# One kernel of attention, routed experts and a SoLU layer: the overflow path moved behind the second layer, and the order inside the attention loop changed

## The chip, the core and the metric

The kernel runs on one core of one Trainium2 chip. The metric is the device time of one execution, in microseconds. A core has five engines that run their own instruction queues and meet through semaphores: TensorE (PE in the profile, PEld for its weight loads), VectorE (DVE), ScalarE (ACT), GpSimd (POOL) and SyncE (SP, which here only issues transfers). Transfers issued by SP or ACT are described in hardware; the scattered row transfers of this kernel are issued by GpSimd, one instruction for 128 rows.

## The reference

```python
for t in range(S):                                   # 2 batches, 8 heads, 768 steps, head size 40
    m_new = maximum(f[t] + m, i[t])
    f_stab, i_stab = exp(f[t] + m - m_new), exp(i[t] - m_new)
    C = f_stab * C + i_stab * outer(v[t], k[t])
    n = f_stab * n + i_stab * k[t]
    y[t] = sigmoid(o[t]) * (C @ q[t]) / maximum(abs(n @ q[t]), 1)
x = y as 1536 rows of 320
logits = x @ w_gate + log1p(exp(x @ w_noise)) * noise
top2 = the two largest of 8 experts; weights by softmax over the two
x = sum over the two: weight * (relu(x @ w1[e]) @ w2[e])       # 320 -> 1024 -> 320
h = x @ w_in; s = h * softmax(h); ln = (s - mean) / sqrt(var + 1e-6) * g
out = ln @ w_out
```

## The kernel before

The work has three stages: attention with routing (0 to 125 us of the profile), eight experts (to about 330 us), the SoLU layer (to the end).

**Attention** works on 12 tiles of 128 tokens, `i` = 0 to 11, two batches in turn, in a loop that is written out and software-pipelined by hand (manual schedule: the order of the calls is the order of each engine's queue). The loop of lines 679 to 718 runs over `i` = 4 to 10; the first tiles are written out ahead of it, and the last (`t` = 11) behind it. One turn `i` does on TensorE, in this order: `ranks(i-3)` (L449, L450), half of the scores of tile `i+1` with `update(i)` between two pairs of them (`scores`, L340; `update`, L368), `inter(i)` (L376, the state part of the output), the other scores, with `attend(i)` (L381, 41 columns per head) in two halves around a pair of scores and `trans(i-1)` (L415), then `logits(i-1)` (L425).

Around it, in the order of their queues:

- GpSimd: `rows` copies one column (L400), `keys(i+1)` makes the decayed queries and the decayed state (L350, L352), `send(i-3)` scatters the rows of a finished tile to its two experts' places in `xg` (two indirect transfers, L473, each behind a one-element memset, L472), and `causal(i+2)` masks the decay matrix `E` (L333). In turns 5, 7 and 9 it also makes the low half of one third of expert 0's first weights (`split_lo`, L121).
- VectorE: `rows(i-1)`, `route(i-2)` and `slot(i-3)` woven together (L401 to L457), `probs(i+1, 0)` (L344: `E` times scores), the keys with their weights (L357), `state(i)` (L391), `probs(i+1, 1)`.
- ScalarE: exponentials (L324, L329), copies of transposes (L419), the high halves of the weights.

Buffers tie the turns together: two PSUM buffers for the scores, so the scores of a tile wait for the `probs` of the tile before it; one PSUM buffer `U`, so `update(i+1)` waits for `state(i)`; four SBUF buffers for the rows `x`, so the copy L400 and the product L405 of `rows(4)` wait until both transfers of `send(0)` have landed.

`send(0)` is issued ahead of the loop (line 663), with `causal(5)` behind it in GpSimd's queue (line 675). It is the first indirect transfer of the program.

**Early rows.** The first 192 rows of expert 0 are complete when tile 7 is sent. They are read back (`early_load`), transposed (`early_turn`, L503), and put through expert 0's first layer (`early_mm`, 8 groups of 8 matmuls, L127 to L134) and most of its second (`early_out`, L149 to L154) while the last tiles are still being routed. `early_cut` (L139 on ScalarE, L140 and L142 on VectorE) takes a group of `early_mm` out of PSUM; the second-layer buffers of `early_out(0)` are those of groups 2 and 3, so it waits for both cuts. `split2(j)`, j = 3 to 6, makes the low half of a piece of expert 0's second weights on VectorE (L121) and issues the load of the next expert's piece. `busy` and `fill` issue matmuls on constant data whose result nobody reads.

**The overflow path.** Experts have fixed row counts (`CAPS`). `totals` (L769 to L774) writes into `cmi` whether any count is exceeded. Lines 803 to 861 load `cmi` into a register of every engine (L803) and branch on it (L804): if it is set, a general path recomputes all experts from all rows with plain loops. With the inputs timed it is skipped. In the kernel before it stands between the attention stage and the experts; what the fast path would write for the same rows is sent out of bounds by adding `flag` to its row numbers (L798 to L800, L974, L975).

## Time and profile before

| | us |
|---|---|
| median of 3 runs | 437.44 (437.33 to 437.52) |
| the execution that was profiled | 438.42 |
| its span, first to last instruction | 436.6 |
| mean granted TensorE clock | 0.963 |

The profile tells for each engine how long it was busy, in what order the work ran, and what ended each wait. The granted clock is given as a share of 2.4 GHz: 1.00 is that, 0.50 is 1.2 GHz. Times below are from the start of the span. A line of the timeline gives start, duration, engine, source line, operation, output and inputs, and in brackets how long the engine was idle before it and what the profile takes to have ended the wait. Where one wait is for several things, the one named is the last by the profile, which need not be the true one.

### The profile page before, as it was taken

What the parts mean: (1) busy time and instruction counts of PE and PEld (TensorE: products, weight loads), DVE (VectorE), ACT (ScalarE), POOL (GpSimd) and SP (SyncE); (2) the same over time, 40 slices, a digit from 0 to 9 for tenths busy, and PEclk for the clock granted to TensorE, in tenths of its full rate; (3) what the DMA queues carried; (4) which work ended last, traced back from release to release, by engine and by line L of the source; (5) the groups of instructions that cost most, each with busy time, mean ns of one, the idle gap of its engine ahead of it and who ended that gap; (6) DMA issues with size and microseconds to landing.
All of it is one profiled execution on the core that took longest, in us unless ns stands there. A gap on an engine that the chain in (4) does not pass through costs nothing.

```text
span 436.6 us, 8125 instructions
## 1 busy us (share of the span) xinstructions
PE 424.3 (97%) x2731; PEld 397.1 (91%) x2731; DVE 291.8 (67%) x736; ACT 242.9 (56%) x524; POOL 203.0 (46%) x284
## 2 busy tenths in 40 slices
PE   7999899999989999999999999999999999999996
PEld 4898799999979999999999999999897898999996
DVE  8897788677646368486585867756656875666541
ACT  4786826753137463663736547373835866656651
POOL 8582798984317443444435345362022543423330
PEclk9999958997699999999999999999999999999999
DMA  6879956955635859376594756736114112210001
GB/s 191 257 228 268 318 187 211 290 224 162 187 111 162 301 173 295 109 262 202 156 298 128 264 187 218 252 98 186 49 60 146 55 47 62 75 45 17 30 17 47
DMA packets 37538, 71.75 MB, mean 164 GB/s; under 512 B 4386, under 2 KB 19142, under 8 KB 37489
## 3 DMA queue, kind: packets, MB, share of 16 engines
q1 hardware_dynamic: 34336, 62.06, 45.5%
q0 software_dynamic: 2912, 8.68, 5.5%
q8 instruction: 24, 0.39, 0.4%
q10 hardware_dynamic: 240, 0.41, 0.3%
q14 instruction: 26, 0.20, 0.2%
HBM read 55.50 MB, written 16.21 MB: 164 GB/s over the span
## 4 chain that ended last, share of the span: by engine, by line
PE 70%; DVE 0%; ACT 0%; issue 0%; DVEq 0%; ACTq 0%
PE po L149 6%; PE po L151 6%; PE po L150 6%; PE ph L127 3%; PE cpo L1162 3%; PE cpo L1164 3%; PE cpo L1163 3%; PE ph L128 3%; PE ph L133 3%; PE ph L132 3%; PE ph L134 3%; PE ph L129 3%; PE ph L130 3%; PE ph L131 3%; PE pt L989 2%; PE pz L1154 2%
## 5 line engine op out<-in xcount | busy, mean ns | idle before, releaser
L121 POOL TENSOR_TENSOR w0l<-r,w0h 128x1024 fp32r<-128x1024 f32 x24 | 57.5, 2394 | 30.7 <-ACT w0h L117 27.5
L166 POOL DMA_INDIRECT yt<-YS,ti x29 | 31.2, 1075 | 86.1 <-ACT YS L164 55.7
L140 DVE SCALAR_TENSOR_TENSOR h<-ph,h 128x384 fp32r<-128x384 f32 (+1 forms) x64 | 34.6, 541 | 54.3 <-ACT h L139 54.3
L149 PE MATMUL po<-w1h,h 128*128 128x320 f32 x184 | 56.7, 308 | 0.0
L151 PE MATMUL po<-w1h,h 128*128 128x320 f32 x184 | 56.7, 308 | 0.0
L150 PE MATMUL po<-w1l,h 128*128 128x320 f32 x184 | 56.6, 308 | 0.0
L139 ACT ACTIVATE h<-ph 128x448 fp32r<-128x448 f32 (+6 forms) x64 | 32.2, 502 | 37.2 <-PE ph L134 32.0
L150 PEld LDWEIGHTS po<-w1l,h 128*128 128x128 f32 x184 | 34.6, 188 | 0.0
L149 PEld LDWEIGHTS po<-w1h,h 128*128 128x128 f32 x184 | 34.5, 188 | 0.0
L151 PEld LDWEIGHTS po<-w1h,h 128*128 128x128 f32 x184 | 34.5, 188 | 0.0
L473 POOL DMA_INDIRECT xg<-x,slots x24 | 25.8, 1076 | 18.2 <-DVE ix L441 6.2
L340 PE MATMUL S<-Qb,Kb 128*128 128x128 f32 x192 | 32.1, 305 | 0.6 <-DVE E L344 0.6
L121 DVE TENSOR_TENSOR w1l<-r,w1h 128x640 fp32r<-128x640 f32 x36 | 29.4, 821 | 2.6 <-ACT w1h L117 2.6
L1156 DVE TENSOR_TENSOR ZL<-pz,ZH 128x512 fp32r<-128x512 f32 x24 | 15.4, 685 | 22.6 <-ACT ZH L1155 22.6
L1162 PE MATMUL cpo<-w1h,ZH 128*128 128x320 f32 x96 | 30.0, 312 | 0.0
L1164 PE MATMUL cpo<-w1h,ZL 128*128 128x320 f32 x96 | 29.7, 310 | 0.0
L1163 PE MATMUL cpo<-w1l,ZH 128*128 128x320 f32 x96 | 29.7, 309 | 0.0
L164 ACT ACTIVATE YS<-po 128x320 f32<-128x320 f32 x20 | 8.8, 439 | 37.2 <-issue 31.1
L117 ACT ACTIVATE w0h<-r 128x1024 fp32r<-128x1024 f32 x27 | 28.2, 1050 | 0.0
L340 PEld LDWEIGHTS S<-Qb,Kb 128*128 128x128 f32 x192 | 26.9, 209 | 1.2 <-DVE E L344 1.0
L117 ACT ACTIVATE w1h<-r 128x640 fp32r<-128x640 f32 x36 | 25.5, 731 | 0.5 <-DMA r<-in_w_dram 0.5
L381 PEld LDWEIGHTS Y<-KV,E 128*128 128x128 f32 x192 | 25.1, 204 | 0.2
(264 smaller groups left out, 1249.7 us busy)
## 6 DMA issues: line engine op xcount, KB each, us to landing
r<-in_w_dram SPq DMA_DIRECT2D x24, 512.0 KB
r<-in_w_dram SPq DMA_DIRECT2D x32, 320.0 KB
E<-gd SPq DMA_DIRECT2D x8, 512.0 KB
X<-xg SPq DMA_DIRECT2D x7, 579.0 KB
KV<-in_kv_dram SPq DMA_DIRECT2D x12, 324.0 KB
cY<-yt SPq DMA_DIRECT2D x12, 320.0 KB
cvR<-in_win_dram SPq DMA_DIRECT2D x6, 512.0 KB
cvR<-in_wout_dram SPq DMA_DIRECT2D x5, 512.0 KB
```

The lines of the kernel that those rows point to most:

```text
L117: act.activation(splits[e][2 * m][:, k : k + n], raws[e, j], AF.Copy)
L121: eng.tensor_sub(splits[e][2 * m + 1][:, k : k + n], raws[e, j], splits[e][2 * m][:, k : k + n].bitcast(F32))
L139: act.activation(h[:, 0:n], ph, AF.Relu)
L140: ve.scalar_tensor_tensor(h[:, n + r : n + r + w], ph[:, 0:w], 0.0, h[:, 0:w].bitcast(F32), op0=ALU.max, op1=ALU.subtract)
L149: pe.matmul(po, hh, W2H[:, f], start=a, stop=False)
L150: pe.matmul(po, hh, W2L[:, f], start=False, stop=False)
L151: pe.matmul(po, hl, W2H[:, f], start=False, stop=z)
L166: i = pool.indirect_dma_start(out=yt, out_offset=bass.IndirectOffsetOnAxis(ap=idx[0:w], axis=0), in_=YS[0:w], in_offset=None, bounds_check ...
L340: pe.matmul(S[:, a], Kb[i % 3][j][:, a], Qb[i % 3][:, a], start=True, stop=True)
L1162: pe.matmul(po, ZH[:, f], W2H[:, f], start=(f == 0), stop=False)
L1163: pe.matmul(po, ZH[:, f], W2L[:, f], start=False, stop=False)
L1164: pe.matmul(po, ZL[:, f], W2H[:, f], start=False, stop=(f == 7))
```

## The change

Three things are done.

1. The overflow path moves to the end of the kernel, behind the last store. It now also recomputes the SoLU layer and writes the output itself, and its direct transfers are issued by GpSimd instead of SP. The `flag` arithmetic of the fast path goes; instead `positive` clears the sign bit of the row numbers (one VectorE instruction beside each `place`).
2. In the attention loop: `send(0)` moves behind `causal(5)`; `attend(i)` is cut into 2, 3 and 3 heads instead of 4 and 4, with a pair of scores between the first two cuts and behind the second; the three `split_lo` on GpSimd become six VectorE subtractions of 512 columns, one in each of the turns 5 to 10, behind `probs(i+1, 1)`; `busy(2)` of turn 9 goes.
3. Behind the loop: `attend(11)` is cut after 3 heads instead of 2; `busy(1)` comes behind it and `busy(2)` behind the `early_turn`s; `split2(3)` moves behind `send(t-1)`; `split2(4)` to `split2(6)` move behind `early_cut(1)` to `early_cut(3)`; `early_cut(0)` moves ahead of `slot(t)` and `totals`.

```diff
+    def positive(ti):
+        ve.tensor_scalar(ti, ti, 0x7FFFFFFF, None, op0=ALU.bitwise_and)
...
         probs(4, 0)
         keys(4)
-        send(0)
         state(3)
...
         load_d(7)
         causal(5)
+        send(0)
         logits(2)
...
             if i > CUT + 1:
                 send(i - 3)
-            if i in (5, 7, 9):
-                split_lo(0, i // 2 - 2, pool)
             if i < CUT + 2:
                 send(i - 3)
             inter(i)
             state(i)
+            attend(i, 0, 2)
             scores(i + 1, 1, 0, 2)
-            attend(i, 0, 4)
+            attend(i, 2, 5)
             scores(i + 1, 1, 2, 4)
             probs(i + 1, 1)
+            if i > 4:
+                j, hs = (i - 5) // 2, slice((i - 5) % 2 * 512, (i - 5) % 2 * 512 + 512)
+                ve.tensor_sub(splits[0][1][:, j, hs], raws[0, j][:, 0, hs], splits[0][0][:, j, hs].bitcast(F32))
             trans(i - 1)
             transc(i - 1)
-            attend(i, 4, 8)
-            if i == 9:
-                busy(2)
+            attend(i, 5, 8)
...
-        attend(t, 0, 2)
+        attend(t, 0, 3)
         trans(t - 1)
         transc(t - 1)
-        attend(t, 2)
+        attend(t, 3)
+        busy(1, "U")
...
         for d in range(3):
             early_turn(d)
             early_split(d)
+        busy(2, "U")
         trans(t)
         transc(t)
         weave(route(t - 1))
-        split2(3)
         early_mm(0)
...
         weave(slot(t - 1))
-        split2(4)
         send(t - 1)
+        split2(3)
         early_mm(2)
         weave(rows2(t), route(t))
-        split2(5)
         early_mm(3)
         ranks(t)
...
+        early_cut(0)
         weave(slot(t), totals())
-        split2(6)
         send(t)
         early_mm(4)
         early_mm(5)
-        for f in range(4):
+        for f in range(1, 4):
             early_cut(f)
+            split2(f + 3)
         early_mm(6)
...
-        ve.tensor_scalar(flag, cmi, 1.0, NONE, op0=ALU.min, op1=ALU.mult)
...
-    rv = nc.values_load(cmi[0:1, 0:1], min_val=0, max_val=NT * NT)
-    with tc.If(rv > 0):
...
             store(t)
+    rv = nc.values_load(cmi[0:1, 0:1], min_val=0, max_val=NT * NT)
+    with tc.If(rv > 0):
...
+                pool.dma_start(W1, w1[bass.ds(e, 1)].rearrange("o p k f -> (o p) k f"))
...
+                pool.dma_start(out[r : r + P], Oo)
```

## Rows read from the trace of the kernel before

**Rows 1.** The page: busy time by engine; granted clock in 40 slices, in tenths.

```profile
PE 424.3 (97%) x2731; PEld 397.1 (91%) x2731; DVE 291.8 (67%) x736; ACT 242.9 (56%) x524; POOL 203.0 (46%) x284
PEclk9999958997699999999999999999999999999999
```

**Rows 2.** Stretches: turns 5, 6, 7, 9, then the stage behind the loop.

```profile
core 0: us, PE busy (x) PEld busy (x) DVE busy (x) ACT busy (x) POOL busy (x), PEclk, DMA share, GB/s
49.88:64.06 14.18, 12.29 (x61) 11.71 (x60) 13.32 (x31) 5.49 (x16) 13.41 (x18) 0.60 0.65 227
64.06:73.18 9.12, 9.12 (x61) 9.07 (x60) 7.14 (x24) 5.45 (x15) 7.75 (x11) 0.69 0.66 211
73.18:79.64 6.46, 6.46 (x61) 6.41 (x60) 4.98 (x24) 5.17 (x16) 5.98 (x8) 1.00 0.91 266
...
86.10:92.86 6.76, 6.76 (x62) 6.62 (x61) 4.65 (x22) 5.77 (x16) 6.29 (x9) 1.00 0.94 345
...
98.57:103.87 5.30, 5.30 (x45) 4.75 (x44) 4.30 (x25) 1.85 (x8) 3.03 (x6) 1.00 0.53 130
103.87:117.49 13.62, 13.62 (x67) 13.35 (x68) 9.85 (x48) 3.52 (x13) 6.00 (x11) 0.50 0.66 206
117.49:123.45 5.96, 5.96 (x44) 5.69 (x43) 1.74 (x13) 0.66 (x2) 0.09 (x1) 1.00 0.38 118
123.45:125.33 1.88, 0.00 (x1) 0.04 (x1) 0.06 (x1) 0.00 (x0) 0.00 (x0) 1.00 0.00 0
```

**Rows 3.** Timeline, turns 4 and 5: how the first send reaches TensorE.

```profile
41.54 2.45 ACT L329 ACTIVATE E<-E,bT 128x128 f32<-128x128 f32 x8
...
45.91 1.41 POOL L473 DMA_INDIRECT xg<-x,slots  x1 [4.25 <-DVE ix L441]
...
47.62 0.96 POOL L473 DMA_INDIRECT xg<-x,slots  x1 [0.21 <-issue]
...
48.59 1.11 POOL L333 TENSOR_SCALAR_AFFINE_SELECT E<-E 128x1024 f32<-128x1024 f32 x1
...
49.74 0.69 DVE L344 TENSOR_TENSOR E<-E,S 128x512 f32<-128x512 f32 x1 [2.82 <-POOL E L333]
...
51.99 0.65 DVE L391 TENSOR_TENSOR CC<-CC,U 40x164 f32<-40x164 f32 x2
...
52.70 1.68 PE L368 MATMUL U<-KV,kw 128*104 128x82 f32 x8 [1.50 <-DVE CC L391]
```

**Rows 4.** Timeline, turn 5: the decayed queries for `inter(5)`.

```profile
49.78 1.27 POOL L350 TENSOR_TENSOR qa<-Qb,A 128x512 f32<-128x512 f32 x1
```

**Rows 5.** Transfers issued from 44 to 46 us: the first send, us to landing.

```profile
xg<-x,slots POOLq DMA_INDIRECT x1, 7.3
```

**Rows 6.** Timeline, turn 7: where `inter` begins at the full clock.

```profile
74.97 1.02 PE L376 MATMUL Y<-CC,qa 128*128 128x82 f32 x8
```

**Rows 7.** Line L121 by engine (min/median/max ns); timeline beside the first on GpSimd.

```profile
L121 DVE TENSOR_TENSOR w1l<-r,w1h x36: 815/820/828, 106.8 to 318.2; 128x640 fp32r<-128x640 f32 x36
...
L121 POOL TENSOR_TENSOR w0l<-r,w0h x24: 2338/2399/2430, 57.5 to 291.3; 128x1024 fp32r<-128x1024 f32 x24
...
57.06 3.14 DVE L405 TENSOR_TENSOR x<-nm,den 128x320 f32<-128x320 f32 x1
```

**Rows 8.** Timeline behind the loop: one cut on VectorE; the load of the remaining rows.

```profile
115.11 0.28 DVE L140 SCALAR_TENSOR_TENSOR eh<-eph,eh 128x128 fp32r<-128x128 f32 x1
...
115.31 0.21 DVE L142 SCALAR_TENSOR_TENSOR eh<-eph,eh 128x64 fp32r<-128x64 f32 x1
...
119.02 0.38 SPq L795 DMA_DIRECT2D rest<-xg  x1
```

**Rows 9.** Line L804, the branch: ns min/median/max, first and last start.

```profile
L804 PEldq COMPARE_BRANCH  x1: 3657/3657/3657, 121.4 to 121.4; - x1
L804 DVEq COMPARE_BRANCH  x1: 72/72/72, 122.3 to 122.3; - x1
...
L804 DVEq EVENT_SEMAPHORE  x1: 21/21/21, 125.2 to 125.2; - x1
```

**Rows 10.** Timeline at the end: ScalarE's last copy, ahead of the last store.

```profile
432.68 0.44 ACT L1170 ACTIVATE O<-cpo 128x320 f32<-128x320 f32 x1 [2.81 <-PE cpo L1164]
```

More of the change, by code (lines that the diff above doesn't have):

```diff
@@ L78, in fused_kernel @@
     eti = cp.tile([P, 2], I32, name="eti")
-    etf = cp.tile([P, 2], F32, name="etf")
     tf = cp.tile([P, 8], F32, name="tf")
@@ L656, in fused_kernel @@
         weave(route(1), slot(0), rows2(2))
-        if 1:
-            exp_a(5)
-        else:
-            exps(5)
+        exp_a(5)
         probs(4, 0)
         keys(4)
-        send(0)
         state(3)
@@ L669, in fused_kernel @@
         transc(2)
-        if 1:
-            exp_e(5)
+        exp_e(5)
         attend(3, 4, 8)
@@ L791, in fused_kernel @@
             early_out(f)
-        place(etf[:, 0:1], early["x"][:, 0:1], 0.0)
-        place(etf[0:64, 1:2], early["x"][0:64, 1:2], 0.0)
+        place(eti[:, 0:1], early["x"][:, 0:1], 0.0)
+        place(eti[0:64, 1:2], early["x"][0:64, 1:2], 0.0)
+        positive(eti[:, 0:1])
+        positive(eti[0:64, 1:2])
         sp.dma_start(rest, xg[EARLY:CAP].rearrange("(n p) d -> p n d", p=P))
         ve.max_index(turn, rank, cnt[:, 2:10])
-        ve.tensor_scalar(flag, cmi, 1.0, NONE, op0=ALU.min, op1=ALU.mult)
@@ L972, in alloc_x @@
             w = float(e) if e < 2 else tf[:, (e - 1) % 6 : (e - 1) % 6 + 1]
-            if e == 0:
-                place(etf[:, 0:m], v["x"][:, 0:m], w)
-                ve.tensor_scalar(v["ti"][:, 0:m], etf[:, 0:m], flag, None, op0=ALU.add)
-            else:
-                place(v["ti"][:, 0:m], v["x"][:, 0:m], w)
+            place(v["ti"][:, 0:m], v["x"][:, 0:m], w)
+            positive(v["ti"][:, 0:m])
             if v["n"] % P:
                 place(v["ti"][0:64, m : m + 1], v["x"][0:64, m : m + 1], w if e < 2 else w[0:64])
+                positive(v["ti"][0:64, m : m + 1])
                 if v["w"][m] < 64:
```

161 lines of the change are left out of this document (103 added, 58 removed).

## The prediction, made before the changed kernel was run

> **What bounds the kernel.** I read the page first. TensorE is busy 97% of the span, no other engine over 67%, so time can only come from three things: less work on TensorE, a higher clock under it, or the few places where it stands still. The clock line is at 9 nearly everywhere, but low in two stretches, around slices 5 to 7 and 10 to 11 [rows 1]. Then I cut the attention stage into stretches [rows 2]. Turn 7 is the reference: 6.46 us, TensorE busy throughout, clock 1.00. Turn 5 takes 14.18 us at a mean of 0.60 and turn 6 takes 9.12 us at 0.69, so these two lose 14.18 + 9.12 - 2 x 6.46 = 10.38 us. Behind the loop, 13.62 us run at 0.50; at twice the clock the same matmuls would take 6.81 us. At the branch TensorE stands still for 1.88 us. From there to the end the clock is up and TensorE is the bound, so an edit counts only as far as it touches these three places or the very end.
>
> Then the timeline ahead of the first fall [rows 3]. The exponentials of tile 5 are done at 41.54 + 2.45 = 43.99, but their mask (48.59) stands behind both transfers of `send(0)` in GpSimd's queue, and the first of these starts only at 45.91, after 4.25 us without work. So `probs(5, 0)` waits 2.82 us for the mask, `state(4)` comes at 51.99, and `update(5)` on TensorE has waited 1.50 us for it when it starts at 52.70. The clock goes to 0.50 at that time.
>
> **The mask ahead of the send.** The mask then runs from 44.0 to 45.1, `probs(5, 0)` loses its 2.82 us, and the waits of TensorE that precede the fall go. With them goes, in the forecast, the low clock of turns 5 and 6: -10.38 us. Two matmuls fewer in turn 9 are worth 6.76 - 6.46 = 0.30 us [rows 2].
>
> What is late next is everything that now stands behind `send(0)`: `keys(5)`, `send(1)`, `causal(6)`, `keys(6)`. The price hangs on the 4.25 us. The profile names an instruction of another tile as what ended it; the second transfer of the same send waits 0.21 us [rows 3]. Two readings bound it. Either the wait belongs to the first indirect transfer of the program and moves with it, or it ends at 45.9 whatever stands in the queue. I take the first, since the rows of the slots that this send needs come from a turn earlier and the second transfer, which reads the same tile, hardly waits. Then:
>
> - `send(0)` starts at 45.1 + 4.25 = 49.4 and its second transfer ends 47.62 + 0.96 - 45.91 = 2.7 us later, at 52.1. The decayed queries of `keys(5)` follow behind a small copy, 52.3 to 53.6, where they ended at 51.05 before [rows 4]. `inter(5)` wants them 74.97 - 73.18 = 1.79 us into its turn [rows 2, 6], at 49.88 + 1.79 = 51.7. TensorE waits 1.9 us.
> - Before, the mask of tile 6 ended some 4.4 us behind these queries; so now at about 58.0. From the start of `probs` to the end of `state` went 51.99 + 0.65 - 49.74 = 2.9 us [rows 3], so `state(5)` ends at 60.9. Turn 6 begins at 49.88 + 6.46 + 1.9 = 58.2 and wants it for its `update` behind a pair of scores: between 0 and 2.7 us of waiting, I take 2.0.
> - `send(0)` took 7.3 us to land [rows 5]. `rows(4)` reuses its buffer, so VectorE stands at L405 until about 51.1 + 7.3 = 58.4 (the second transfer's landing), with `probs(6, 0)` queued behind it, and `trans(4)` on TensorE waits too. That falls into the same 2 us; I add nothing.
>
> Together 3.9 us come back, 0 by the second reading. The loop is worth -10.38 - 0.30 + 3.9 = -6.8 us, between -6 and -10.7.
>
> **The splits.** GpSimd loses three instructions of 2.40 us, VectorE gains six of 512 columns, 0.82 x 512 / 640 = 0.66 us each [rows 7]. In turn 7 VectorE is busy 4.98 of 6.46 us [rows 2], so 0.66 fits into the 1.48 us left: 0. If it did not, 6 x 0.66 = 4.0 us. On GpSimd nothing on the path waits for the room that this makes; beside the first of the three a product on VectorE took 3.14 us [rows 7], which goes away but lay in the slow stretch already counted.
>
> **The order of scores and `attend`** changes no instruction: 0 by count. What it does to the clock no row shows; that is a rival below.
>
> **Behind the loop.** From 98.57 to the first matmul behind the branch at 125.33 are 26.76 us. If the clock holds, 6.81 us go, the branch's 1.88 go, and three `busy` matmuls add 3 x 0.15 (half of turn 9's 0.30 each). TensorE alone would then be through at 98.57 + 26.76 - 6.81 - 1.88 + 0.45 = 117.1. But VectorE does not get faster with the clock. In the two stretches from 103.87 to 123.45 it is busy 9.85 + 1.74 = 11.6 us [rows 2]. `early_out(0)` needs `early_cut(3)`, and in the new order two of the splits stand between the cuts ahead of it. Behind `early_cut(3)` remain one split (0.82) and four cuts of 0.28 + 0.21 = 0.49 [rows 7, 8]: 2.8 us. So 8.8 us of VectorE's work precede it. Of its 13.62 - 9.85 = 3.8 us of waiting I keep half, since part of it was waiting for slow matmuls: `early_cut(3)` ends at 103.87 + 0.45 + 8.8 + 1.9 = 115.0. TensorE's remaining work (six `early_out`, one `early_mm`) is about the stretch that took 5.96 us at full clock [rows 2], less a few matmuls: 5.6. The first matmul of the next stage comes at 120.6 instead of 125.33: -4.7 us, between -3 and -8.2. It needs the load of the remaining rows, issued at 119.02 before [rows 8], behind the last send; the sends hang on the same VectorE chain, and I count on it being there. Each us that it is later costs one.
>
> **The branch at the end.** Nothing runs behind it, but every engine must pass it before the program ends. DVE's branch starts at 122.3 and its next instruction at 125.2; TensorE's has a record of 3.66 us, begun 2.05 us ahead of the end of its last matmul (123.45) [rows 2, 9]. At the end, ScalarE's last copy ends at 433.12, 3.5 us ahead of the span's end [rows 10]; these go to the last store and the closing handshake. Ends: 0, if all of it lies in this tail, and 3.66, if one engine pays it behind everything else. I take 0.5: DVE and GpSimd are done well before, and of TensorE's 3.66 the overlap leaves 1.6, less than the tail.
>
> By the Trainium skill (Runtime: NRT & Kernel Launch, section "Instruction fetch mechanics") a taken branch whose target lies outside the fetched pages stops the engine until the target has been fetched. The trace agrees with the 2.9 us on DVE. Where that is paid is rival 5.
>
> **Signs cleared (`positive`)**: some dozen VectorE instructions of about 0.2 us among the experts, where the clock is 1.00 and TensorE never waits for the row numbers: 0; the `flag` arithmetic that goes is worth as little.
>
> **Sum.** -6.8 - 4.7 + 0.5 = -11.0 us. The profiled execution took 438.42 us, 0.98 above the median, so it would take 427.4, and the median 437.44 - 11.0 = 426.4 us. With the terms' ends, 420.5 to 431.
>
> **Rivals.**
>
> 1. The 4.25 us do not move with the send. `keys(5)` is in time, only L405 waits for the landing (45.91 + 7.3 = 53.2) by about 1 us: loop -9.7, total 423.5. For it: the wait's named end at 45.9. Against: no data of this send are that late.
> 2. The second fall stays. TensorE was busy 5.30 of 5.30 us ahead of it [rows 2], so it does not come from idling, and 0.45 us of added matmuls may be too little. Then behind the loop only 1.88 - 0.45 = 1.4 us are gained: 437.44 - 6.8 - 1.4 + 0.5 = 429.7. The Trainium skill (TensorE: Matmul & The Clock Gate, section "HAM oscillation — how this bites in real kernels") has the clock fall for idle gaps between bursts of matmuls; the trace agrees at the first fall and not at the second. By that rule nothing in the change touches the second, and this rival is its result.
> 3. Slower: the new wait at `inter(5)`, with the late `trans(4)`, brings the clock down near 56 to 60 us, and it does not come back inside the loop. Before, it came back in turn 6: a mean of 0.69 over 9.12 us is 3.5 us at 1.00, so 5.6 us into the turn, behind an unbroken run of scores, `update`, scores, `inter`, scores. The change breaks that run with two heads of `attend`. A turn at 0.50 takes at least 64.06 - 52.70 = 11.36 us. Turns 6 to 10: 5 x (11.36 - 6.46) = 24.5; loop 24.5 + 3.9 - 10.7 = +17.7; the 5.30 us behind it double, less 1.4 at the branch, plus 0.5: +22.1, 459.5 us. It decides when the clock is at 0.50 at 62 us.
> 4. The change does not do what it says: the clock falls near 52 us as before and returns in turn 6. 437.44 - 0.3 - 4.7 + 0.5 = 432.9.
> 5. The fetch behind the branch is paid in full at the end: 3.66 instead of 0.5, 429.6.
>
> **Chances.** Forecast 0.47; rival 1 0.17; rival 2 0.13; rival 3 0.12; rival 4 0.07; rival 5 0.04. From 420.5 to 431.5 lie the forecast and rivals 1, 2 and 5, some 0.79; rivals 3 and 4 stay outside. A measurement of this kernel can tell about 0.2% from no change. Faster 0.86 (all but rival 3, less a little for sums that cancel), same 0.02, slower 0.12.
>
> **What would show it.** Right: the mask of tile 5 at 44 to 45 us, `update(5)` without a wait, clock 1.00 from 46 to 100, turns 7 to 10 at 6.5 us or less; a wait of `inter(5)` for L350 near 2 us; VectorE's cuts, not the matmuls, ahead of the first `early_out`; no gap at 123; the span's end some 4 us behind the last copy. Wrong: 0.50 in a turn that was at 1.00, VectorE or GpSimd ending waits of TensorE in turns 7 to 10 (the splits not hidden), or transposes of the remaining rows that wait for their load.

## The result

| | before | changed |
|---|---|---|
| median of seven executions | 438.19 | 435.03 |
| lowest | 437.33 | 431.91 |
| the execution that was profiled | 438.42 | 435.03 |
| its span | 436.6 | 433.4 |
| mean granted clock | 0.963 | 0.975 |

The change gains: ratio 0.988 (95% interval 0.984 to 0.992), 5.2 us of 438; the medians differ by 3.2. The forecast was a gain of 11.0. The ratios here and below leave out executions more than 1.5% above the fastest of their kernel; medians keep them, which is why some medians and ratios do not match.

The page of the changed kernel, beside [rows 1]: TensorE is as full as before, VectorE busier (69%), GpSimd less so.

```profile
PE 421.1 (97%) x2732; PEld 391.1 (90%) x2732; DVE 298.3 (69%) x754; ACT 242.5 (56%) x524; POOL 196.4 (45%) x281
PEclk9998999995899999999999999999999999999999
```

The dent of slices 6 and 7 is gone; a small one has come at slice 4, and the one behind the loop is still there. By turns (5, 6, 7, 8, 9, and then from the ranks of turn 11 to the first layer-1 matmul of the experts; columns as in [rows 2]):

```profile
50.49:57.17 6.68, 6.65 (x60) 6.48 (x59) 3.95 (x17) 5.46 (x16) 6.14 (x11) 1.00 0.96 331
57.17:66.16 8.99, 7.25 (x60) 6.64 (x59) 8.86 (x31) 5.46 (x16) 7.90 (x11) 1.00 0.84 286
66.16:73.68 7.52, 6.86 (x61) 6.52 (x60) 7.41 (x26) 5.18 (x16) 5.50 (x9) 1.00 0.89 252
73.68:81.99 8.31, 8.28 (x61) 8.11 (x60) 8.16 (x27) 5.45 (x16) 6.27 (x10) 0.79 0.88 280
81.99:88.66 6.67, 6.64 (x60) 6.47 (x59) 6.56 (x25) 5.35 (x16) 4.64 (x8) 1.00 0.84 267
94.82:125.07 30.25, 27.84 (x172) 25.01 (x172) 18.33 (x98) 7.65 (x27) 9.49 (x20) 0.77 0.54 166
```

Turn 5 went from 14.18 to 6.68 us, without the wait of 1.9 that the forecast had in it. Turn 6, forecast at 6.46 + 2.0, is 8.99, and turns 7 and 8, which were to be 6.5 each, are 7.52 and 8.31 (in turn 8 the clock, at 0.79, has a part in it). In these three VectorE (the fourth figure) is busy for all but 0.1 to 0.15 us; in turn 7 of [rows 2] it had 1.48 us to spare. The whole loop, turns 4 to 10, and the stage behind it:

```profile
42.74:98.57 55.83, 53.60 (x408) 52.39 (x407) 43.28 (x171) 34.48 (x100) 46.60 (x62) 0.85 0.76 247
98.57:127.48 28.91, 27.03 (x169) 25.98 (x169) 17.15 (x93) 7.53 (x27) 9.12 (x17) 0.76 0.52 152
```

This is the kernel before; the changed one has

```profile
43.59:94.82 51.23, 48.65 (x407) 46.51 (x406) 47.12 (x172) 34.35 (x100) 39.74 (x58) 0.97 0.81 261
```

So the loop gives 4.6 us (forecast 6.8), and the stage behind it takes 30.25 - 28.91 = 1.3 us back (forecast a gain of 4.7). Two small pieces complete the 3.2 us between the two spans: the loop begins 0.85 us later (43.59 instead of 42.74, with the dent of slice 4 ahead of it), and from the first layer-1 matmul of the experts to the end it takes 308.3 us instead of 309.1. These are one execution of each kernel. Three places of the timeline of the changed kernel carry the rest of the text. First, the send and the mask, beside [rows 3 to 6]:

```profile
44.91 1.09 POOL L336 TENSOR_SCALAR_AFFINE_SELECT E<-E 128x1024 f32<-128x1024 f32 x1 [2.91 <-ACT z L432]
46.26 1.23 POOL L476 DMA_INDIRECT xg<-x,slots  x1 [0.23 <-DVE den L407]
...
51.09 0.88 PE L371 MATMUL U<-KV,kw 128*104 128x82 f32 x8
...
54.37 0.49 DVE L408 TENSOR_TENSOR x<-nm,den 128x320 f32<-128x320 f32 x1 [2.13 <-DMA xg<-x,slots]
```

The mask comes at 44.9, `update(5)` no longer waits, the send follows with 0.23 us of idle time, and L408 (L405 before) waits for its landing. Second, the VectorE splits (L703) and GpSimd's instructions beside them:

```profile
59.34 1.10 POOL L336 TENSOR_SCALAR_AFFINE_SELECT E<-E 128x1024 f32<-128x1024 f32 x1
...
59.54 2.85 DVE L703 TENSOR_TENSOR w0l<-r,w0h 128x512 fp32r<-128x512 f32 x1
...
60.52 1.26 POOL L353 TENSOR_TENSOR qa<-Qb,A 128x512 f32<-128x512 f32 x1
61.75 1.23 POOL L355 TENSOR_TENSOR CC<-CC,A 128x328 f32<-128x328 f32 x1
...
67.02 2.88 DVE L703 TENSOR_TENSOR w0l<-r,w0h 128x512 fp32r<-128x512 f32 x1
...
74.52 2.87 DVE L703 TENSOR_TENSOR w0l<-r,w0h 128x512 fp32r<-128x512 f32 x1
...
94.48 0.68 DVE L703 TENSOR_TENSOR w0l<-r,w0h 128x512 fp32r<-128x512 f32 x1
```

The same instruction takes 0.68 us with GpSimd at rest and 2.85 to 2.88 beside its mask and keys. Third, the load of the remaining rows, the transposes that want it, and ScalarE's last copy, beside [rows 8, 10]:

```profile
118.99 0.38 SPq L797 DMA_DIRECT2D rest<-xg  x1
...
122.92 0.85 PE L924 MATMUL pt<-consts,rest 128*128 128x128 f32 x6 [1.42 <-DMA rest<-xg]
...
429.76 0.44 ACT L1105 ACTIVATE O<-cpo 128x320 f32<-128x320 f32 x1 [3.08 <-PE cpo L1099]
```

### The profile page after: what moved, and what is told of

Read it like the earlier page. It is cut to its first block, busy times and chain, and to the rows that moved or that the text cites. A ratio compares the mean times of both kernels' runs of the same rounds, so it can differ in the third digit from the quotient of the medians.

```text
span 433.4 us, 8131 instructions
## 1 busy us (share of the span) xinstructions
PE 421.1 (97%) x2732; PEld 391.1 (90%) x2732; DVE 298.3 (69%) x754; ACT 242.5 (56%) x524; POOL 196.4 (45%) x281
## 4 chain that ended last, share of the span: by engine, by line
PE 80%; DVE 13%; DMA 3%; issue 2%; ACT 1%; POOL 0%; POOLq 0%; DVEq 0%; ACTq 0%
PE po L149 6%; PE po L148 6%; PE po L150 6%; PE ph L126 4%; PE cpo L1099 3%; PE cpo L1098 3%; PE cpo L1097 3%; PE ph L127 3%; PE ph L129 3%; PE ph L131 3%; PE ph L133 3%; PE ph L132 3%; PE ph L128 3%; PE ph L130 3%; PE pt L924 3%; DMA xg<-x,slots 2%
## 5 line engine op out<-in xcount | busy, mean ns | idle before, releaser
L120 POOL TENSOR_TENSOR w0l<-r,w0h 128x1024 fp32r<-128x1024 f32 x21 | 50.4, 2400 | 30.4 <-ACT w0h L116 30.1
L476 POOL DMA_INDIRECT xg<-x,slots x24 | 25.6, 1066 | 21.6 <-DVE slots L460 5.6
L343 PE MATMUL S<-Qb,Kb 128*128 128x128 f32 x192 | 30.7, 295 | 0.7 <-DVE E L347 0.7
L343 PEld LDWEIGHTS S<-Qb,Kb 128*128 128x128 f32 x192 | 25.4, 199 | 1.3 <-DVE E L347 1.1
L384 PE MATMUL Y<-KV,E 128*128 128x41 f32 x192 | 25.6, 279 | 0.0
```

Of the source, the lines that this page charges most:

```text
L120: eng.tensor_sub(splits[e][2 * m + 1][:, k : k + n], raws[e, j], splits[e][2 * m][:, k : k + n].bitcast(F32))
L343: pe.matmul(S[:, a], Kb[i % 3][j][:, a], Qb[i % 3][:, a], start=True, stop=True)
```

## Experiments

### The send alone, and everything but the send

```diff
 (the kernel before)                     (the changed kernel)
         keys(4)                              keys(4)
-        send(0)                         +    send(0)
...
         causal(5)                            causal(5)
+        send(0)                         -    send(0)
```

> The kernel before with one part of the change alone: send(0) behind causal(5). Theory (the send's move is what pays in the loop): the mask of tile 5 at 45 us, update(5) without its wait, turns 5 and 6 together 14 to 15 us instead of 23.3, time 428 to 430. Then the rest of the change costs some 5 us. Rival (the first fall needs the other order too): the clock falls near 50 us all the same, 436 to 438.

> The changed kernel with one part undone: send(0) ahead of the loop as in the kernel before, behind keys(4). Theory (the prediction's first term): the mask of tile 5 again stands behind the send at 48 to 49 us, TensorE waits ahead of update(5), the clock is at 0.50 in turns 5 and 6, and the loop is longer by 5 to 9 us: 440 to 444. Of the start wait: the send again begins near 45.9 us behind some 4 us without work, since in the trace of after it began at 46.26 with only 0.23 us of waiting. Rival (the first fall of the clock has another cause and is gone by the new order of attend and scores): the same late mask, but the clock stays at 1.00 from 50 to 60 us and the time is 435 to 437.

The send alone: ratio to before 0.997 (0.994 to 1.000). Everything but the send: 0.998 (0.996 to 1.000). Both together, the change, 0.988. The send back in its old place brings the old picture:

```profile
46.10 1.34 POOL L476 DMA_INDIRECT xg<-x,slots  x1 [4.38 <-DVE ix L444]
...
48.73 1.10 POOL L336 TENSOR_SCALAR_AFFINE_SELECT E<-E 128x1024 f32<-128x1024 f32 x1
49.86 0.69 DVE L347 TENSOR_TENSOR E<-E,S 128x512 f32<-128x512 f32 x1 [2.82 <-POOL E L336]
...
52.82 1.11 PE L371 MATMUL U<-KV,kw 128*104 128x82 f32 x8 [1.50 <-DVE CC L394]
```

with turn 5 at 13.23 us and a mean clock of 0.62. So the late mask makes the first fall with either order of `attend`, and the 4.38 us do not move with the instruction: the send starts at 46.10 here, 45.91 before, 46.26 in the changed kernel, and in its variants between 46.07 and 47.16 (in one, in which the clock was low ahead of the loop, right behind its mask at 51.29). What ends at about 46 us no trace names; that stays open. Why the send alone gains so little is read in part from its trace, just before TensorE's next turn:

```profile
54.92 0.49 DVE L405 TENSOR_TENSOR x<-nm,den 128x320 f32<-128x320 f32 x1 [2.46 <-DMA xg<-x,slots]
...
57.35 2.34 POOL L121 TENSOR_TENSOR w0l<-r,w0h 128x1024 fp32r<-128x1024 f32 x1
57.45 2.27 DVE L444 TENSOR_TENSOR mk<-oh 128x8 bf16<-128x8 f32 x1
...
59.77 0.19 PE L449 MATMUL pr<-mk,ltri 128*128 128x8 bf16 x1 [2.12 <-DVE mk L444]
```

L405 waits for the landing, so the routing behind it runs late, and one of its small sums (0.17 us elsewhere) starts 0.1 us behind GpSimd's split and takes 2.27. TensorE waits 2.12 us for it, and the next turn runs at a mean of 0.71: turns 5 and 6 take 9.05 and 10.03 us. The whole loop is still 3.6 us shorter than before (52.2 instead of 55.8); but the stage behind it, which this edit does not touch, takes 31.2 us in this trace instead of 28.9, and the loop begins 0.84 us later, so nearly all of the gain is gone.

### The splits, and the landing

Back on GpSimd in turns 5, 7 and 9:

```diff
-            if i > 4:
-                ve.tensor_sub(splits[0][1][:, j, hs], ...)
...
+            if i in (5, 7, 9):
+                split_lo(0, i // 2 - 2, pool)
```

> The changed kernel with one part undone: the low halves of expert 0's first weights are again three instructions on GpSimd in turns 5, 7 and 9. Theory (the splits on VectorE cost turns 6 to 10): in the trace of after each split of 512 columns ran beside GpSimd's tensor instructions and took 2.2 to 2.9 us five times of six, VectorE was busy 7.4 of 7.51 us in turn 7 and set its length. So turns 7 and 8 go from 7.51 and 8.31 to about 6.5, turn 6 from 8.99 to about 8, and the time from 435.0 to 431 or 432. Rival (turns 6 to 8 are long because the first send lands late and L408 waits for it, and because of a short fall of the clock; the splits fit): the turns stay, 435 within 1 us.

On VectorE, but ahead of `probs(i + 1, 0)`:

```diff
             scores(i + 1, 0, 2, 4)
+            if i > 4:
+                ve.tensor_sub(...)
             probs(i + 1, 0)
```

> The changed kernel with the six VectorE splits kept, each moved ahead of probs(i+1, 0), a place where GpSimd is issuing its sends and runs no tensor instruction. Theory: each split takes 0.66 to 0.7 us instead of 2.2 to 2.9, VectorE is busy 5.6 us of a turn, turns 7 to 9 take 6.5 us, the time is 431 to 432. Rival 1 (late landing and clock): splits short or not, turns 6 to 8 stay, 435. Rival 2 (these splits are slow in themselves, for their strided operands): 2.2 us or more in the new place as well, and 435 or above.

Six buffers for `x`, alone and with each of the others:

```diff
-            xx = T[i]["x"] = a4.tile([P, XR + 1], F32, tag="x", name=f"x{i}")
+            xx = T[i]["x"] = a4.tile([P, XR + 1], F32, tag="x", name=f"x{i}", bufs=6)
```

> The changed kernel with six buffers for the rows x instead of four, and nothing else, so that the product L408 of rows(4) no longer waits for the landing of send(0). Theory (the landing is what the move of the send costs: L408 waits 2.1 us until 54.4, trans(4) and the rest of the turn's routing are late and fall beside GpSimd's tensor instructions, TensorE stands still near 57 us, and a clock at 0.50 often begins there): L408 at about 51.5, no gap of TensorE over 0.5 us from 54 to 60, turn 6 at 7.5 us (then still set by the VectorE splits) instead of 8.99, time 432 to 433.5. Rival (the landing is hidden, the splits alone set turns 6 to 8): 434.5 to 435.5.

> Six buffers for x and the VectorE splits moved ahead of probs(i+1, 0), clear of GpSimd's tensor instructions. Theory (both are needed: the landing opens the gap near 57 us, the splits beside GpSimd lengthen turns 6 to 9): splits 0.68 us, no gap of TensorE over 0.7 us between 50 and 90 us, clock 1.00 through turns 5 to 10, each of 6.5 us, the loop ends near 90.5 us instead of 94.4, time 430 to 431.5. Rival (the clock falls in the loop whatever is done): a stretch at 0.50 between 55 and 90 us, 434 to 438.

> The kernel before with send(0) behind causal(5) and six buffers for x; splits, order and overflow path as before. Theory (the send's move pays only when its landing holds nobody up): no gap over 0.5 us near 57 us, clock 1.00 in turns 5 to 10 (6.5 to 7 us each), the loop ends near 90 us, time 428 to 432. Rival (GpSimd's split beside the rows and keys opens the gap near 57 us by itself, with 2.3 us on VectorE): the clock falls near 58 us as with the send alone, 436 to 438.

With six buffers and the splits on GpSimd in turns 7, 8 and 9:

```diff
+            if i in (7, 8, 9):
+                split_lo(0, i - 7, pool)
```

> The changed kernel with six buffers for x, and the splits back on GpSimd but one each in turns 7, 8 and 9, so that no split stands on either engine in turns 5 and 6. Theory (an instruction of VectorE with both operands in SBUF waits for the end of GpSimd's run of tensor instructions; every gap of TensorE near 57 to 69 us in the runs so far begins with one such wait of 2.2 to 3.2 us, of L703, L447, L360 or L394's forerunners; with a shorter run of GpSimd in turns 5 and 6 it ends before TensorE needs it): no gap of TensorE over 1 us from 50 to 92 us, turns 5 to 10 of 6.2 to 6.8 us each, loop ends near 89 us, time 430. Rival (one VectorE instruction is caught by GpSimd's run anyway, and the clock falls in the loop): a gap of 2 us or more between 55 and 75 us with 0.50 behind it, 435 to 441.

| kernel | ratio to before (95%) | executions in the ratio | median of all, that of before beside it |
|---|---|---|---|
| changed | 0.988 (0.984 to 0.992) | 6 of 7 | 435.03, 438.19 |
| splits on GpSimd | 0.992 (0.988 to 0.996) | 7 of 8 | 434.88, 439.27 |
| splits ahead of `probs` | 0.987 (0.983 to 0.991) | 4 of 10 | 437.89, 439.27 |
| six buffers | 0.991 (0.987 to 0.995) | 8 of 10 | 436.49, 439.47 |
| six buffers, splits ahead of `probs` | 0.988 (0.982 to 0.993) | 3 of 10 | 440.30, 439.47 |
| kernel before, send moved, six buffers | 0.998 (0.994 to 1.001) | 10 of 10 | 439.11, 439.47 |
| six buffers, splits on GpSimd in 7, 8, 9 | 0.986 (0.979 to 0.993) | 3 of 5 | 434.17, 438.79 |

None is told from the changed kernel by its ratio, save the kernel before with send and buffers changed, which is no faster than before; the ratios with 3 or 4 executions of 10 speak for few of them, and by the medians of all executions the two kernels with the splits ahead of `probs` gain 1.4 us and nothing. Each of these edits was expected to bring the time to 428 to 433.5 (the single theory that it tested), and none did by its median; so by the times every theory of a single cause falls, mine first. What a split on VectorE costs the whole time is therefore not shown; that it is held is shown by the durations: ahead of `probs` all six splits take 0.68 us (the line by itself; ns min/median/max), so they are not slow in themselves.

```profile
L690 DVE TENSOR_TENSOR w0l<-r,w0h x6: 682/684/685, 57.6 to 97.8; 128x512 fp32r<-128x512 f32 x6
```

But then some other instruction of VectorE meets GpSimd's run. In the kernel before with send and buffers changed it is the keys' product in turn 6, beside GpSimd's split again:

```profile
56.48 2.83 DVE L357 TENSOR_TENSOR kw<-KV,wS 128x160 f32<-128x160 f32 x2
56.56 2.34 POOL L121 TENSOR_TENSOR w0l<-r,w0h 128x1024 fp32r<-128x1024 f32 x1
...
59.94 1.27 PE L368 MATMUL U<-KV,kw 128*104 128x82 f32 x6 [2.62 <-DVE CC L391]
```

The tensor instructions that are caught have both operands in SBUF (L703, L444, L357); those with one in PSUM keep their time (L347 0.69, L394 0.65 in all these traces). A copy and a cast with a single operand, in SBUF, are caught too: L412 takes 1.29 us at 54.90 in the changed kernel (0.19 elsewhere), and the cast L460, 0.15 us elsewhere, is shown below. The Trainium skill (SBUF — State Buffer, section "Who interferes with whom") says that a VectorE instruction with two SBUF inputs contends with a GpSimd instruction that reads SBUF, and that the later one is blocked until the first is done. The trace agrees, and goes further: L703 at 59.54 stands through the mask and L353, its own 0.6 us follow L353's end, and L355 behind it takes 1.23 instead of 0.73. At 67.02 it stands through L355 as well and ends at 69.90, 0.57 us behind it. So a run of GpSimd instructions back to back holds VectorE for more than one instruction, at most to the end of the run.

Six buffers did take away the wait at L408 (no wait, 51.81), but turn 6 still took 8.33 us instead of 8.99: the split is short there (0.72), and the cast is held instead.

```profile
59.77 2.58 DVE L460 CAST slots<-sf 128x2 int32<-128x2 f32 x1
...
60.36 1.27 POOL L353 TENSOR_TENSOR qa<-Qb,A 128x512 f32<-128x512 f32 x1
61.58 0.73 POOL L355 TENSOR_TENSOR CC<-CC,A 128x328 f32<-128x328 f32 x1
```

And with one split in each of three successive turns GpSimd (the last busy figure) and VectorE between them set the turn, 7.83 and 8.20 of 8.31 us; 3.67 us of VectorE's are the same cast, held until the split has ended:

```profile
65.37:73.68 8.31, 6.84 (x60) 6.50 (x59) 8.20 (x25) 5.17 (x16) 7.83 (x10) 1.00 0.81 243
```

### The clock behind the loop

Twelve `busy` matmuls instead of three:

```diff
         attend(t, 0, 3)
+        busy(4, "U")
         trans(t - 1)
...
-        busy(1, "U")
+        busy(2, "U")
...
         logits(t - 1)
+        busy(3, "U")
...
-        busy(2, "U")
+        busy(3, "U")
         trans(t)
```

> As the kernel with six buffers and the moved splits, and twelve instead of three busy matmuls behind the loop (four ahead of trans(10), two behind attend(11), three behind logits(10), three behind the early_turns). Theory (the second fall is answered by TensorE's own work in the stage: with more matmul columns in it the clock holds): clock 1.00 from 90 to 120 us, the stage is shorter by up to 6.8 us less 1.7 us of added matmuls, of which the chain of routing takes back a part: 2 to 4 us below the kernel without them. Rival (the second fall comes whatever TensorE does there): 0.50 for 13.7 us again, time equal or up to 2 us longer.

> The same with twelve busy matmuls behind the loop instead of three. In the kernel with the moved splits the twelve kept the clock at 1.00 from 97 us to the end, and from ranks of turn 11 to the first layer-1 matmul of the next stage went 26.1 us instead of 30.1. Theory (the second fall is decided by TensorE's work in that stage): 4 us less than the kernel with three, 426 to 427. Rival (it was chance): the second fall is there again, time equal or 1 us longer.

> The changed kernel with one thing altered, twelve busy matmuls behind the loop instead of three. Theory (the second fall is decided by TensorE's work in that stage, and costs some 4 us net): clock 1.00 from 96 us on, from the ranks of turn 11 to the first layer-1 matmul of the experts 26 us instead of 30.25, time 430.5 to 431.5. Rival (what the fall costs is hidden behind the routing of the last tiles and the load of the remaining rows): the wait for that load grows from 1.4 to 5 us, time within 1 us of the changed kernel.

The stage in the last of these (the changed kernel with nothing else altered), and in the kernel with six buffers and splits in turns 7 to 9:

```profile
99.01:126.96 27.95, 25.27 (x182) 22.51 (x182) 17.91 (x96) 7.67 (x27) 9.05 (x17) 0.94 0.57 173
```

```profile
99.82:126.76 26.94, 23.68 (x182) 20.92 (x181) 17.28 (x94) 7.65 (x27) 9.09 (x17) 1.00 0.58 179
```

30.25 us at 0.77 become 27.95 at 0.94 and 26.94 at 1.00. In the traces of six kernels with the twelve the stage takes 25.6 to 27.95 us, at means of 0.94 to 1.00; in four of the changed kernel and its variants with three, 28.7 to 31.2, at 0.67 to 0.83. So the second fall answers to TensorE's own work there, and what it costs is 1 to 5 us net of the nine added matmuls. It is not bound to come without them: in the kernel before with send and buffers changed the clock stayed up until the last 4 us of the stage, which took 27.8. As times: 0.989 (0.982 to 0.997) for the busy matmuls alone (expected 430.5 to 431.5, median 435.51), no difference that can be told from 0.988; in this trace turn 6 took 13.05 us at a mean of 0.52 and the gain is hidden behind that. With six buffers and the splits on GpSimd, 0.984 (0.981 to 0.987; expected 426 to 427, median 433.11). The kernel with six buffers, the splits ahead of `probs` and the twelve gave 0.988 (0.980 to 0.995).

### The changed kernel a second time

> The changed kernel unaltered, for a second trace of it. If the places of the low clock are set by the program, they are those of the first trace (32.7, 73.7 and 97.6 us); if they depend on how an execution happens to fall against the clock's control, the short ones move or vanish and the one behind the loop stays; the turns with VectorE's splits beside GpSimd (7.5 us) are the same in both cases. Time 434 to 436.

Turns 5, 6, 7 and the stage behind the loop (the first layer-1 matmul starts at 129.28, 0.1 us behind the end of the last stretch), and then the place where turn 5 loses its time:

```profile
50.18:60.22 10.04, 8.15 (x61) 7.87 (x60) 7.39 (x24) 5.48 (x16) 9.26 (x16) 0.82 0.93 318
60.22:72.38 12.16, 12.16 (x61) 12.05 (x60) 7.81 (x27) 5.46 (x15) 7.41 (x11) 0.50 0.52 160
72.38:81.25 8.87, 8.84 (x61) 8.67 (x60) 7.44 (x24) 5.14 (x15) 5.62 (x8) 0.74 0.71 215
...
100.55:129.18 28.63, 27.74 (x172) 26.14 (x172) 17.57 (x94) 7.65 (x27) 9.10 (x17) 0.76 0.53 169
```

```profile
54.04 2.74 DVE L408 TENSOR_TENSOR x<-nm,den 128x320 f32<-128x320 f32 x1 [2.01 <-DMA xg<-x,slots]
...
54.48 1.25 POOL L353 TENSOR_TENSOR qa<-Qb,A 128x512 f32<-128x512 f32 x1
...
56.93 0.87 PE L418 MATMUL pT<-consts,x 128*128 128x128 f32 x3 [1.89 <-DVE x L445]
```

The same program, much the same wait for the landing (2.01 us, 2.13 in the first trace); but in this execution L408 is released at 54.04, while GpSimd's mask is still running, and is held for 2.74 us. In the first trace it started at 54.37 and got through in 0.49, ahead of the keys. TensorE then waits 1.89 us, the clock goes to 0.50 and stays through turn 6: 439.6 us against 435.0 (on a chip where the kernel before has a median of 440.5 against 438.2). L408 starts 0.11 us ahead of the mask's end in the one and 0.35 us in the other. So the falls in the loop do not belong to the program alone; by these two traces a few tenths in a landing can decide, which no run tests by itself. Four times of this kernel on this chip ran from 433.8 to 441.4 (ratio 0.989, 0.982 to 0.996).

### The overflow path back in between

The whole `If` block moved back behind the early rows, in the kernel with six buffers, splits on GpSimd in turns 7 to 9 and twelve busy matmuls.

> The same again, with the overflow path (its new text) back between the attention stage and the experts. Theory (the path costs its gap where it stands and next to nothing at the end): TensorE stands still for about 1.9 us at the branch, time 0.5 to 2 us above the kernel with the path at the end; the tail behind the last copy is as long as before, 3.5 us against 3.2. Rival 1 (the branch is hidden behind the load of the remaining rows, for which TensorE waits anyway): equal within 0.5 us. Rival 2 (the fetch is paid in full at the end): the path in between is faster.

0.985 (0.979 to 0.991) against 0.984 (0.981 to 0.987) with the path at the end. The transposes of the remaining rows, first with the path at the end, then with it between (with the load that they want):

```profile
124.61 0.85 PE L925 MATMUL pt<-consts,rest 128*128 128x128 f32 x6 [2.62 <-DMA rest<-xg]
```

```profile
115.96 0.38 SPq L798 DMA_DIRECT2D rest<-xg  x1
...
121.51 0.85 PE L1035 MATMUL pt<-consts,rest 128*128 128x128 f32 x6 [3.04 <-DVE wts L914]
```

TensorE waits 2.6 to 3.0 us there in either case, once for the load and once with the branch inside the wait. The two times lie 0.4 us apart with intervals of over 1 us to each side, so they do not decide between the theory and rival 1. By the traces the branch is hidden only in part: in the other kernels with the twelve the transposes begin 3.3 to 4.3 us after the load was issued, which here would be by 120.3, and they begin 1.2 us or more later. At the end of the kernel the branch shows as little: from the end of the last copy to the end of the span 2.8 us without it and 3.2 with it.

### All together

The changed kernel with six buffers, splits on GpSimd in turns 7, 9 and 10, `attend` in its old halves of four, twelve busy matmuls:

```diff
+            if i in (7, 9, 10):
+                split_lo(0, (i - 6) // 2, pool)
...
-            attend(i, 0, 2)
             scores(i + 1, 1, 0, 2)
-            attend(i, 2, 5)
+            attend(i, 0, 4)
...
-            attend(i, 5, 8)
+            attend(i, 4, 8)
```

> The changed kernel with six buffers for x, the splits on GpSimd in turns 7, 9 and 10 (not in turns that follow one another: in 7, 8 and 9 each turn took 8.3 us, with 8.1 us of work on GpSimd), the old order of attend (4 and 4 heads, the scores ahead), and twelve busy matmuls behind the loop. Theory (four separate terms): turns without a wait go from 6.68 to 6.46 us by the order alone; no gap of TensorE over 1 us in turns 5 to 10, loop ends near 89 us; clock 1.00 behind it and 26 us from ranks of turn 11 to the next stage; time 425 to 428. Rival (some instruction of VectorE is caught by GpSimd's run in turn 5 or 6 whatever is done, and the clock falls): a gap of over 1.2 us near 57 or 70 us, 0.50 behind it, 431 to 436.

0.983 (0.975 to 0.990); expected 425 to 428, median 433.93. Turn 7, and the stage behind the loop:

```profile
72.65:79.11 6.46, 6.46 (x60) 6.41 (x60) 5.82 (x23) 5.17 (x16) 5.98 (x8) 1.00 1.06 281
...
99.75:125.38 25.63, 23.67 (x181) 20.90 (x181) 17.38 (x94) 7.67 (x27) 10.01 (x20) 1.00 0.60 188
```

A turn without a wait takes 6.46 us with four heads behind `trans` and 6.68 with three. Here the clock was low before turn 5 instead (0.50 in the 8 us ahead of the loop), so two more kernels got matmuls on constant data at the weak places there and in the loop: this one, and the changed kernel with its waits left in.

```diff
         attend(2, 0, 4)
-        fill(2, "D")
+        fill(4, "D")
         attend(2, 4, 8)
-        fill(2, "D")
+        fill(4, "D")
...
+            if i in (4, 5, 6, 9, 10):
+                busy(2)
             trans(i - 1)
```

> The combined kernel (six buffers for x, splits on GpSimd in turns 7, 9 and 10, old order of attend, twelve busy matmuls behind the loop) with fourteen more matmuls on constant data at the places where an execution so far lost the clock: four behind the two halves of attend(2) ahead of the loop, and two ahead of trans in turns 4, 5, 6, 9 and 10. They cost up to 14 x 0.19 = 2.7 us of TensorE where they do not fall into a wait. Theory (the clock falls where TensorE's own work is thin, and what the change can bring depends on it): no stretch at 0.50 from 15 to 430 us, ranks of turn 11 near 90 us, the next stage 26 us later, 425 to 427, and the times of single executions within 3 us of each other instead of 6 to 20. Rival (the falls come for another reason): stretches at 0.50 in the loop as before, and the added matmuls on top, 433 to 436.

> The changed kernel with the same matmuls on constant data added, nine behind the loop and fourteen ahead of and in it, and nothing else altered: splits beside GpSimd, four buffers for x and the new order of attend stay. Theory (two sorts of loss: the clock, and VectorE held by GpSimd): the clock holds at 1.00, but turns 6 to 8 still take 7.5 us or more and TensorE waits near 57 us; so 3 to 4 us above the combined kernel, 428 to 431. Rival (only the clock matters): equal to the combined kernel within 1.5 us.

The first, combined with all the rest: 0.980 (0.972 to 0.988), median 429.91 (expected 425 to 427) where the kernel before had 439.92, lowest 428.64. It has the lowest ratio and median of the study, though its interval overlaps those of the others; three of its five times lie within 1.3 us and two are 5 to 7 us above these. Its page, its turn 6 and the stage behind:

```profile
PEclk9999989999999999999999999999999999999999
```

```profile
57.21:66.42 9.21, 8.88 (x62) 8.39 (x62) 8.57 (x31) 5.47 (x16) 8.59 (x14) 0.81 0.87 309
...
92.91:119.23 26.32, 23.86 (x182) 20.84 (x182) 18.58 (x94) 7.67 (x27) 11.18 (x20) 1.00 0.59 188
```

The changed kernel with the waits left in: 0.983 (0.977 to 0.989), median 433.59 (expected 428 to 431), and turn 6

```profile
57.64:70.45 12.81, 12.12 (x62) 11.30 (x61) 12.44 (x33) 5.48 (x16) 10.91 (x16) 0.60 0.62 215
```

The two medians differ by 3.7 us, as the theory of two sorts of loss expected, but the intervals overlap, and neither kernel held the clock through turn 6. That both sorts are needed is borne out by the traces, not settled by the times.

## Why the prediction was wrong, step by step

The spans differ by 3.2 us where 11.0 were forecast. Of the missing 7.8 us, 6.0 lie in the stage behind the loop (forecast -4.7, measured +1.3), 2.2 in the loop (-6.8, -4.6) and 0.85 ahead of it, where the forecast had nothing; the rest of the kernel comes out 1.3 better than forecast. So three steps of the sum failed: the condition "if the clock holds", together with the load that was counted on behind the loop; the splits, booked at nothing; and the order of `attend`, booked at nothing. That these losses are there is shown by durations in the traces; how much of the whole time each is worth is not shown, since undoing or mending one of them moved no median as far as expected.

**The mask ahead of the send: right.** Mask at 44.9 instead of 48.6, `update(5)` without a wait, turn 5 at 6.68 us and 1.00. The send put back restores the fall.

**The 4.25 us that move with the send: wrong.** The send starts at about 46 us whether it stands ahead of the mask or behind it. Rival 1 had the mechanism. So `keys(5)` came at 48.91, not 52.3, and `inter(5)` did not wait. The 3.9 us that I took off for this were spent all the same, and 2.2 more, by other things; that the two sums are of a like size is luck.

**The landing of `send(0)`: named, and booked at nothing.** I had VectorE at L405 until 58.4, "into the same 2 us". It stood until 54.37, and what it costs depends on what the routing behind it runs into. In the first trace TensorE loses 8.99 - 7.25 = 1.7 us in turn 6, in part to this; in the second 1.9 us in turn 5, and the clock with it.

**The splits: the term that was mis-sized.** I priced a split at 0.66 us, scaled from rows of the expert stage, and compared it with 1.48 us of VectorE's slack. Measured: 2.85, 2.88, 2.87, 2.19, 2.68, and 0.68 for the one with GpSimd at rest, 14.15 us instead of 3.96 (in the second trace, with longer turns, 2.88, 0.68, 0.73, 1.86, 0.69 and 0.69). The slack of [rows 2] lay where GpSimd was at work (in that turn VectorE is idle for 1.00 us beside its split and for 0.37 beside its mask and keys), and that is just when VectorE's instructions on two SBUF operands are held. The row that said so was in [rows 7] (3.14 us beside the split on GpSimd); I used it for the split that left and not for the six that came. In turns 6 to 8 a split then begins every 7.5 us, 1.04 above the turn of 6.46. That is the cost in this trace; putting the splits back on GpSimd gave no gain (0.992), since other instructions are held then.

**The order of `attend`: booked at nothing, costs 0.22 us a turn.** Same instructions, same count. The reason is argued from the rows: from the first transpose to the first logits matmul (copies on ScalarE in between) pass 1.14 us in the kernel before and 1.12 in the changed one, and three heads fill less of that than four. 6.68 against 6.46, in six turns some 1.3 us.

**Behind the loop: the condition "if the clock holds" failed.** Rival 2, at 0.13, is what happened: the three busy matmuls were too few. Forecast 4.7 us gained, measured 1.3 lost in the first trace and 0.2 gained in the second (the kernel before with the send moved has 31.2 there, with six buffers as well 27.8, so one trace of each is a rough measure). Where twelve hold the clock at 1.00 the stage is 25.6 to 27.3 us, about 2 to 3 us below the kernel before and not 4.7, because of the second condition, "I count on it being there". The load of the remaining rows was issued at 118.99 as before (119.02), though the stage began 3.75 us earlier: 24.2 us into it instead of 20.5; TensorE waits 1.4 us for it. With the twelve and the path at the end it is issued 19.7 to 21.5 us into the stage, TensorE waits 1.4 to 2.6 us for it, and the transposes begin 23.5 to 24.8 us into it; the forecast had them at 120.6 - 98.57 = 22.0. So once the clock holds, the chain that issues the load, and not TensorE, sets the length.

**The branch at the end: small, as taken.** I took 0.5; from the end of the last copy to the end of the span are 433.4 - 430.2 = 3.2 us where they were 3.5, and 2.8 in the variant with the path back in between. In its old place part of it lies in the wait for the load, which the forecast did not have, so its 1.88 us were not all to be gained.

**Rival 3** was priced too high and drawn from the wrong wait, but its kind is real: the second trace of the changed kernel loses the clock near 56 us and has it back only in turn 7. By that trace the trigger was L408, released by the landing and held by GpSimd, and not `inter(5)`.

**The range** missed because the forecast and rivals 1, 2 and 5 all had the loop at -6.8 us or better and the stage behind it at a gain; none let two steps fail together, or a fall that is removed come back elsewhere. The traces show it coming back in the loop or ahead of it. The range is also not what the terms' ends add up to: 437.44 - 10.7 - 8.2 = 418.5 and 437.44 - 6 - 3 + 3.66 = 432.1; 435.03 lies outside that too. And a measurement tells less than the 0.2% that I counted on: the intervals here are 0.2 to 0.8% to each side.

## What to carry to other kernels

Slack of one engine is worth what the work put there costs beside its neighbour: take the duration from a row in which the other engine runs the same kind of work, and look at whether VectorE's idle time coincides with GpSimd's run. A gain that hangs on TensorE's clock is a gain of an execution, not of the program, as long as other executions lose the clock elsewhere; look at two traces before one fall is put down to one wait. And where a stage ends with a load, price the chain that issues the load before the matmuls ahead of it.

## What the runs showed of the hardware

- VectorE's instructions with both operands in SBUF are held by a back-to-back run of GpSimd's, not by one instruction: 2.2 to 2.9 us for one of 0.68, and 2.27 for one of 0.17. A cast with its one operand in SBUF is held as well (2.58 and 3.67 us for 0.15), and GpSimd's next instruction can be held in turn (1.23 instead of 0.73).
- The clock fell at a place where TensorE was busy 5.30 of 5.30 us [rows 2], and stayed up when nine matmuls on constant data were added to the stage (means of 0.67 to 0.83 in four traces with three, 0.94 to 1.00 in six with twelve).
- Executions of one kernel differ by up to 10 us (431.9 to 441.9 for the changed one), and two of its traces show the low clock in different turns.
